# Attention of a three-stage kernel: a turn's first scores in two halves of the queries, and one turn with its products in another order

## The chip, the cores and the metric

The kernel runs on one core of a Trainium2 chip. The metric is the device time of one execution in microseconds (us); of several runs the median is given.

## The reference, cut to what matters

Three stages follow one another: an attention with fading scores and no softmax, and two feed-forward layers over its output.

```
scores = q @ k.T / sqrt(64)                      # 4 batches, 8 heads, 576 positions, 64 wide
ret    = scores * gamma_h ** (i - j) for i >= j  # else 0
x      = (ret @ v) as 2304 tokens x 512
x      = prelu(x @ w_in, alpha) @ w_out          # 512 -> 2048 -> 512
out    = silu1.702(x @ w2_in) @ w2_out           # h * sigmoid(1.702 h)
```

Inputs and outputs are float32. The change is in the attention alone.

## The kernel before, in words

**The attention's tiling.** The 32 pairs of batch and head are worked two heads at a time: 16 turns, one for each entry of `PAIRS`. A turn's two heads lie in the two halves of the 128 partitions (`halves`, 0 to 63 and 64 to 127). The 576 positions are cut into four chunks of 128 and a tail of 64. Within a chunk the scores are computed and multiplied by a table of fades; across chunks the sum of keys times values is carried as a state, as a linear attention does.

**A turn's products on TensorE**, all made by the helper `mm` (L353), in program order:

- `a_scores` writes the tiles `sc`, one for each head: for each of four chunks and each head one product, weights 64 rows x 128 columns (the keys), 128 queries streamed. The two heads use different row halves of the array.
- `a_outer` writes `st`: keys times values of each chunk, weights 128 x 64. The keys come from `kts`, which `a_keys` has scaled on ScalarE (two instructions, one for each head, L317) after its DMA.
- `a_within` writes `av` of the turn before: the faded scores `r` times the values, weights 128 x 64, 128 queries streamed.
- `a_tail` (tile `st`), then `a_across` (tile `av`), weights 64 x 64: the tail's state, and states times queries for the turn before.

The first turn (i = 0) and the second (i = 1) differ: turn i = 0 does its own `a_within`, and turn i = 1 does none. "The fourth turn" is i = 3.

**Beside them**: `a_evac` (VectorE, L385) multiplies `sc` by the table into `r`; `a_states` and `a_sums` (ScalarE, VectorE) turn `st` into the states that `a_across` of the next turn reads; `a_out` copies the result away; GpSimd scales the queries (`a_queries`). `sc` has three buffers, `av` two.

**What sets the order.** The order on each engine is that in which the program issues instructions (`manual_schedule`). Between the steps of a turn `run_to` issues what is due of a list of events: the loading and the splitting of the first layer's weights. After 16 turns and one more for the rest come the first layer (L514, L555) and the second (L696), whose products follow one another in fixed order.

An `mm` on float32 leaves two product records (MATMUL) and two weight-load records (LDWEIGHTS) in the trace, so the 8 products of a turn's scores are 16 records of each kind. The products of the two heads run side by side, so the 16 records come in 8 pairs.

Of the kernel before, what the change touches and what calls it, by code (L numbers as in the profile page):

```python
# [46 lines left out]
def kernel(  # L47
# [68 lines left out]
    def run_to(time):  # L116
        while events and events[0][0] <= time:
            _, _, fn, args = events.pop(0)
            fn(*args)
# [180 lines left out]
    halves = (slice(0, 64), slice(64, 128))  # L300
# [32 lines left out]
    def a_tables(p):  # L333
        def table(o, c0, n, row, key):
            nc.vector.scalar_tensor_tensor(
                out=tab_sb[o, p, c0:c0 + n], in0=row, scalar=vtab_sb[o, p, key:key + 1],
                in1=mask_sb[o, o.start:o.start + n], op0=ALU.mult, op1=ALU.mult,
            )

        for e in range(2):  # L340
            table(slice(0, 128), e * 128, 128, query(p, e), e)
        for e, o in enumerate(halves):
            table(o, 256, 64, query(p, e, o, 64), 4)

    def a_otab(p):
        for e, o in enumerate(halves):
            copy(tab_sb[o, p, 320:448], query(p, e, o))
        o = tab_sb[:, p, 320:768]
        copy(o[:, 128:256], o[:, 0:128])
        copy(o[:, 256:448], o[:, 0:192])  # L350

    def mm(out, lhsT, rhs, start, stop):
        return nc.tensor.matmul(  # L353
            out=out, lhsT=lhsT, rhs=rhs, start=start, stop=stop, skip_group_check=True
        )

    def a_keys(i):
        n = kts(i).rearrange("p (j n) -> p j n", j=4)
        for e, o in enumerate(halves):
            scale(n[:, :, o], n[:, :, o], vtab_sb[:, PAIRS[i][1], e:e + 1])  # L360
        k_t[i] = n

    def a_scores(i, chunks=range(4)):
        q, k = ld[i][0:2]
        if i not in sc_t:
            sc_t[i] = [aps.tile([128, 512], F32, tag="sc", name="sc", bufs=3) for _ in halves]
        t = sc_t[i]
        for j in chunks:
            for e, o in enumerate(halves):
                mm(t[e][:, j * 128:j * 128 + 128], k[j][o], q[j][o], j == 0, True)  # L370

    def a_tail(i):
        q, k = ld[i][0:2]
        for o in halves:
            mm(s_t[i][o, 0:64], k[4][o], q[4][o], i == 0, True)

    def a_outer(i):
        t, v, n = s_t[i], ld[i][2], k_t.pop(i)
        for j in range(4):
            for e, o in enumerate(halves):  # L380
                mm(t[o, j * 64 + 64:j * 64 + 128], n[:, j, o], v[:, 2 * j + e], i > 0 and j == 0, True)

    def a_evac(i):
        for e, t in enumerate(sc_t.pop(i)):
            nc.vector.tensor_tensor(  # L385
                out=r_t[i][0][:, e].rearrange("p (j n) -> p j n", j=4),
                in0=t.rearrange("p (j n) -> p j n", j=4),
                in1=tab_sb[:, PAIRS[i][1], e * 128:e * 128 + 128].rearrange(
                    "p (a n) -> p a n", a=1).to_broadcast([128, 4, 128]),
                op=ALU.mult,  # L390
            )

    def a_queries(i):
        behind = latest[0]
        r = tmp("r", i, [128, 2048])
        r_t[i] = (
            r[:, 0:1024].rearrange("p (e n) -> p e n", e=2), r[:, 1024:1536],
            r[:, 1088:1600].rearrange("p (b n) -> p b n", b=2)[:, :, 0:64], r[:, 1600:2048],
        )
        ins = nc.gpsimd.tensor_tensor(  # L400
            out=r_t[i][3], in0=ld[i][3], in1=tab_sb[:, PAIRS[i][1], 320:768], op=ALU.mult
        )
        if behind:
            tc.add_manual_dep(ins.ins, behind.ins.name, SYNC, reason="beside the products of the scores")

    def a_states(i):
        p = PAIRS[i][1]
        s = r_t[i][1]
        scale(s[:, 0:320], s_t.pop(i)[:, 0:320], vtab_sb[:, p, 2:3])

    def a_sums(i):
        p = PAIRS[i][1]
        s = r_t[i][1]
        nc.vector.scalar_tensor_tensor(
            out=s[:, 320:512], in0=s[:, 64:256], scalar=vtab_sb[:, p, 2:3], in1=s[:, 128:320],
            op0=ALU.mult, op1=ALU.add,
        )
        half = r_t[i][2]
        nc.vector.scalar_tensor_tensor(
            out=s[:, 384:512].rearrange("p (b n) -> p b n", b=2), in0=half,  # L420
            scalar=vtab_sb[:, p, 3:4], in1=s[:, 384:512].rearrange("p (b n) -> p b n", b=2),
            op0=ALU.mult, op1=ALU.add,
        )
        latest[0] = nc.vector.tensor_tensor(
            out=s[:, 0:64], in0=s[:, 0:64], in1=tab_sb[:, p, 256:320], op=ALU.mult
        )

    def a_within(i):
        v, r = ld[i][2], r_t[i][0]
        t = aps.tile([128, 1024], F32, tag="av", name="av", bufs=2)  # L430
        av_t[i] = t, [t[:, A0 + j * 128:A0 + j * 128 + 128] for j in range(4)] + [t[:, A0 + 512:A0 + S]]
        for j in range(4):
            for e, o in enumerate(halves):
                mm(av_t[i][1][j][o], v[:, 2 * j + e], r[:, e, j * 128:j * 128 + 128], j % 2 == 0, True)

    def a_across(i):
        out, v = av_t[i][1], ld[i][2]
        _, s, _, q = r_t.pop(i)
        for c in range(1, 5):
            s0 = 64 if c == 1 else 192 + c * 64  # L440
            for o in halves:
                mm(out[c][o], s[o, s0:s0 + 64], q[o, c * 128 - 128:min(c * 128, 448)], False, True)
        for o in halves:
            mm(out[4][o], v[o, 8], s[o, 0:64], False, True)

    def a_out(i):
        b, p = PAIRS[i]
        t = av_t.pop(i)[0][:, A0:A0 + S]
        ld.pop(i)
        s0 = 0  # L450
        for c in range(2):
            n0, n1 = max(CH[c][0] - b * S, 0), min(CH[c][1] - b * S, S)
            if n0 >= n1:
                continue
            if (c, p) not in x_t:
                x_home(c, p, xp[c])
            o = b * S - CH[c][0]
            x = x_t[c, p][:, :, n0 + o:n1 + o]
            copy(x[:, 0], t[:, n0:n1])
            rests.append((x, t[:, n0:n1]))  # L460
            s0 = n1
        if s0 < S:
            n = i - NP
            if n // 3 not in xs_t:
                xs_t[n // 3] = tmp("xs", n // 3, [128, 3, S])
            copy(xs_t[n // 3][:, n % 3, s0:S], t[:, s0:S])
# [3 lines left out]
    def a_rests():  # L470
        while rests:
            x, t = rests.pop(0)
            sub(nc.vector, x[:, 1], t, x[:, 0])
# [452 lines left out]
    with tc.manual_schedule():  # L926
# [24 lines left out]
        for i in range(n_a + 1):  # L951
            j = i - 1
            if i < n_a:
                a_scores(i)
                a_queries(i)
                a_evac(i)
            if i in (1, 2):
                a_tables(i + 1)
            a_rests()
            run_to(i)  # L960
            if i < n_a:
                s_t[i] = aps.tile([128, 512], F32, tag="st", name="st")
                if i == 0:
                    a_tail(i)
                a_outer(i)
                if i == 0:
                    a_states(i)
                    a_tables(1)
            if i != 1:
                a_within(max(j, 0))  # L970
            if 0 < i < n_a:
                a_tail(i)
                a_states(i)
            if i < n_a:
                a_sums(i)
            if i + 1 < n_a:
                a_keys(i + 1)
            if i == 0:
                a_otab(1)
            run_to(i + 0.25)  # L980
            if i:
                a_across(j)
                a_out(j)
            if i in (1, 2):
                a_otab(i + 1)
            for n in (3, 4) if i == 0 else (i + 4,):
                if n < n_a:
                    a_load(n)
            if i == 0:
                nc.sync.dma_start(out=alpha_sb, in_=alpha)  # L990
            run_to(i + 0.75)
# [49 lines left out]
        for r in range(R):  # L1041
            z = r * 2 * NU
            for j in range(NJ):
                u = z + 7 * j
                for t, what in (
# [3 lines left out]
                    if r == 0 and j in (5, 6) and what in ("g22", "g12"):  # L1049
                        t = 8.01  # L1050
# [114 lines left out]
```

## Time and profile before

| what | value |
|---|---|
| median of 3 runs | 800.93 us (800.91 to 801.43) |
| the profiled execution | 800.28 us, of which its span 798.6 us |
| TensorE busy, products | 793.6 us, 99% of the span |
| TensorE busy, weight loads | 740.2 us, 93% |
| VectorE, ScalarE, GpSimd busy | 80%, 66%, 10% |
| turns 2 to 16 of the attention | from 9.12 us to 63.59 us |

The span runs from the first instruction of the profile to the last one; the execution is 1.7 us longer than it. Product records of TensorE are pipelined and their ends are modelled, so a record's start says more than its length. "Chain" is the work that ended last, followed back from the last instruction. In the chain a piece of an engine is listed from the end of the piece before it.

### The profile page before, as it was taken

The page shows a single profiled execution, that of the slowest core. Times are in us where ns is not written, and L with a number is a line of the kernel's source. Part 1 is how long each engine was busy: PE and PEld are TensorE (multiplying, and loading weights), DVE is VectorE, ACT ScalarE, POOL GpSimd, SP SyncE. Part 2 cuts the span into 40 slices and gives each one's busy share as a digit, 9 for nine tenths or more (in the row PEclk, how much of TensorE's full clock was granted, in tenths as well). Part 3 has the DMA queues.
Part 4 walks back from the last instruction along what each step waited for, and adds up shares of the span by engine and source line. Part 5 has one row for each costly group of instructions (what it writes and reads, how often), then busy time and mean ns, then how long its engine had stood idle before and what let it go on. Part 6 is the DMA issues. An engine that isn't in the chain of part 4 may idle for free.

```text
span 798.6 us, 14132 instructions
## 1 busy us (share of the span) xinstructions
PE 793.6 (99%) x5004; PEld 740.2 (93%) x5004; DVE 642.1 (80%) x1195; ACT 527.9 (66%) x959; POOL 83.5 (10%) x104
## 2 busy tenths in 40 slices
PE   9999999999999999999999999999999999999998
PEld 8998888888888888999999999999999999999997
DVE  7888987888467576879999899799677898787775
ACT  7689869885536856556678666676566675666552
POOL 2230112100022003626100000000000000000000
PEclk9999999999999999999999999999999999999999
DMA  9998999755889966797989556986435985536771
GB/s 351 417 386 333 327 352 342 286 217 209 294 278 401 360 224 227 253 337 254 337 323 355 177 174 233 343 295 235 147 125 193 323 312 187 159 120 232 267 278 60
DMA packets 87789, 214.08 MB, mean 268 GB/s; under 512 B 7971, under 2 KB 43811, under 8 KB 79014
## 3 DMA queue, kind: packets, MB, share of 16 engines
q1 hardware_dynamic: 80784, 187.99, 65.6%
q0 software_dynamic: 6784, 25.17, 9.0%
q8 instruction: 39, 0.64, 0.3%
q14 instruction: 32, 0.26, 0.1%
q10 hardware_dynamic: 150, 0.02, 0.0%
HBM read 152.59 MB, written 60.56 MB: 267 GB/s over the span
## 4 chain that ended last, share of the span: by engine, by line
PE 98%; DMA 1%; DVE 0%; issue 0%
PE acc L696 33%; PE h L696 25%; PE acc L555 16%; PE h L514 16%; PE av L353 4%; PE sc L353 2%; PE st L353 2%; DMA ws<-sm 1%; PE wps L942 0%; PE dq L326 0%; DVE c L178 0%; DVE wz L930 0%
## 5 line engine op out<-in xcount | busy, mean ns | idle before, releaser
L108 DVE TENSOR_TENSOR gsf<-g,gsf 128x384 fp32r<-128x384 f32 (+1 forms) x272 | 156.4, 586 | 54.5 <-ACT gsf L103 53.1
L103 ACT ACTIVATE gsf<-g 128x384 fp32r<-128x384 f32 (+1 forms) x272 | 145.8, 542 | 75.6 <-PE acc L696 32.8
L555 PE MATMUL acc<-gsf,wo 128*128 128x512 f32 x576 | 138.2, 389 | 0.0
L514 PE MATMUL h<-x,wi 128*128 128x512 f32 x576 | 138.2, 389 | 0.0
L696 PE MATMUL acc<-gsf,ws 128*128 128x384 f32 x768 | 135.1, 334 | 0.2 <-DMA ws<-sm 0.2
L696 PEld LDWEIGHTS acc<-gsf,ws 128*128 128x128 f32 x768 | 133.2, 188 | 0.5 <-ACT x L103 0.5
L555 PEld LDWEIGHTS acc<-gsf,wo 128*128 128x128 f32 x576 | 108.1, 188 | 22.8 <-ACT raw L103 0.3
L514 PEld LDWEIGHTS h<-x,wi 128*128 128x128 f32 x576 | 108.1, 188 | 22.5
L696 PE MATMUL acc<-x,ws 128*128 128x384 f32 x660 | 128.3, 334 | 0.0
L696 PEld LDWEIGHTS acc<-x,ws 128*128 128x128 f32 x660 | 115.5, 188 | 0.2 <-ACT tm L103 0.2
L696 PE MATMUL h<-x,ws 128*128 128x384 f32 x540 | 107.7, 334 | 0.0
L696 PE MATMUL h<-gsf,ws 128*128 128x384 f32 x576 | 101.9, 334 | 0.0
L696 PEld LDWEIGHTS h<-gsf,ws 128*128 128x128 f32 x576 | 100.0, 188 | 0.2 <-issue 0.2
L696 PEld LDWEIGHTS h<-x,ws 128*128 128x128 f32 x540 | 94.8, 188 | 0.0
L178 DVE TENSOR_TENSOR tm<-h,tm 128x384 f32<-128x384 f32 x97 | 53.6, 553 | 26.9 <-PE h L696 21.5
L178 DVE TENSOR_TENSOR g<-g 128x384 f32<-128x384 f32 x114 | 63.0, 553 | 0.7
L103 ACT ACTIVATE tm<-acc 128x384 f32<-128x384 f32 x62 | 30.4, 491 | 48.0 <-PE acc L696 46.4
L522 DVE SCALAR_TENSOR_TENSOR g<-g,rise_sb,h 128x512 f32<-128x512 f32 (+1 forms) x49 | 36.4, 742 | 29.7 <-ACT g L527 29.5
L527 ACT ACTIVATE g<-h 128x512 f32<-128x512 f32 (+1 forms) x49 | 29.1, 593 | 40.5 <-PE h L514 39.9
L178 DVE TENSOR_TENSOR raw<-raw 128x256 f32<-128x256 f32 x116 | 45.6, 433 | 1.0
L148 DVE SCALAR_TENSOR_TENSOR raw<-raw 128x1024 int32<-128x1024 int32 x32 | 39.3, 1229 | 2.6 <-ACT raw L141 2.6
L129 POOL DMA_DIRECT2D raw<-in_w_dram x44 | 23.2, 534 | 173.2 <-DVE raw L178 52.9
(104 smaller groups left out, 922.9 us busy)
## 6 DMA issues: line engine op xcount, KB each, us to landing
ws<-sm SPq DMA_DIRECT2D x32, 1024.0 KB, 7.0
ws<-sp SPq DMA_DIRECT2D x24, 1024.0 KB, 5.5
raw<-in_w_dram POOLq DMA_DIRECT2D x44, 512.0 KB, 7.5
sm<-raw SPq DMA_DIRECT2D x32, 512.0 KB, 4.3
pad<-rg SPq DMA_DIRECT2D x48, 256.0 KB, 2.7
ld<-in_qkv_dram SPq DMA_DIRECT2D x13, 864.0 KB, 7.9
raw<-in_w_dram SPq DMA_DIRECT2D x20, 512.0 KB, 8.9
r<-raw SPq DMA_DIRECT2D x16, 512.0 KB, 2.9
```

Of the source, the lines that this page charges most:

```text
L103: return nc.scalar.activation(out=out, in_=in_, func=ACTF.Copy)
L108: latest[0] = eng.tensor_tensor(out=out, in0=a, in1=b.bitcast(F32), op=ALU.subtract)
L129: eng.dma_start(out=raws[key][:, c * DM:c * DM + DM], in_=f[:, c * DM:c * DM + DM])
L148: latest[0] = nc.vector.scalar_tensor_tensor(out=g[:, 0:2 * DM], in0=t[:, :, 1], scalar=3, in1=t[:, :, 0], op0=ALU.logical_shift_left, op1 ...
L178: latest[0] = (eng or nc.vector).tensor_tensor(out=out, in0=x, in1=y, op=op)
L353: return nc.tensor.matmul(out=out, lhsT=lhsT, rhs=rhs, start=start, stop=stop, skip_group_check=True)
L514: nc.tensor.matmul(out=t, lhsT=w[:, cw, k * 128:k * 128 + 128], rhs=x[:, cx], start=(i == 0), stop=(i == 3 * NK - 1),)
L522: nc.vector.scalar_tensor_tensor(out=g[0], in0=g[1], scalar=rise_sb[:, m:m + 1], in1=h, op0=ALU.mult, op1=ALU.add)
L527: nc.scalar.activation(out=out, in_=in_, func=ACTF.Relu, scale=-1.0)
L555: nc.tensor.matmul(out=acc[0][d], lhsT=w[:, d // 2, cw, d % 2 * 128:d % 2 * 128 + 128], rhs=g[:, cx], start=(m == m0 and i == 0), stop=(m ...
L696: nc.tensor.matmul(out=out, lhsT=w(cw), rhs=x(cx), start=(start and n == 0), stop=True, skip_group_check=True,)
```

## The change

Two edits. In `a_scores`, for the first chunk of every turn but the first, each head's product of 128 queries is issued as two products of 64: first both heads on queries 0 to 63, then both heads on queries 64 to 127, with the same keys as weights. The flag that starts a new sum in the PSUM bank stays on the first half alone. In turn i = 3 `a_within` is issued in front of `a_outer` and not behind it.

```
         for j in chunks:
-            for e, o in enumerate(halves):
-                mm(t[e][:, j * 128:j * 128 + 128], k[j][o], q[j][o], j == 0, True)
+            for cols in halves if j == 0 and i else (slice(0, 128),):
+                for e, o in enumerate(halves):
+                    n = slice(j * 128 + cols.start, j * 128 + cols.stop)
+                    mm(t[e][:, n], k[j][o], q[j][o, cols], j + cols.start == 0, True)
...
                 if i == 0:
                     a_tail(i)
+                if i == 3:
+                    a_within(j)
                 a_outer(i)
...
-            if i != 1:
+            if i not in (1, 3):
                 a_within(max(j, 0))
```

TensorE at the head of turn i = 4, which stands for the turns i = 1 to 15, before (a shape is that of the output: partitions x columns):

```order
L353 MATMUL av<-r,ld 64x64 x2
L353 MATMUL sc<-ld 128x128 x8
L353 MATMUL st<-ld,kts 64x64 x8
L353 MATMUL av<-r,ld 64x128 x8
L353 MATMUL st<-ld 64x64 x2
```

The same place with the change:

```order
L353 MATMUL av<-r,ld 64x64 x2
L353 MATMUL sc<-ld 128x64 x4
L353 MATMUL sc<-ld 128x128 x6
L353 MATMUL st<-ld,kts 64x64 x8
L353 MATMUL av<-r,ld 64x128 x8
```

Two products of 128 queries have become four of 64; the six of the other chunks stand as before.

TensorE in turn i = 3, before (in brackets the engine or the DMA queue whose semaphore an instruction waits for):

```order
L353 MATMUL sc<-ld 128x128 [waits DMAHW4_49]
L353 MATMUL sc<-ld 128x128 [waits DVE_49]
L353 MATMUL sc<-ld 128x128 x6
L353 MATMUL st<-ld,kts 64x64 [waits DMAHW5_49,PE_49,Activation_49]
L353 MATMUL st<-ld,kts 64x64 [waits Activation_49]
L353 MATMUL st<-ld,kts 64x64 x6
L353 MATMUL av<-r,ld 64x128 [waits DVE_49]
L353 MATMUL av<-r,ld 64x128 x7
L353 MATMUL st<-ld 64x64 x2
```

The same turn with the change:

```order
L353 MATMUL sc<-ld 128x64 [waits DMAHW4_49]
L353 MATMUL sc<-ld 128x64 [waits DVE_49]
L353 MATMUL sc<-ld 128x64 x2
L353 MATMUL sc<-ld 128x128 x6
L353 MATMUL av<-r,ld 64x128 [waits DVE_49]
L353 MATMUL av<-r,ld 64x128 x7
L353 MATMUL st<-ld,kts 64x64 [waits DMAHW5_49,PE_49,Activation_49]
L353 MATMUL st<-ld,kts 64x64 [waits Activation_49]
L353 MATMUL st<-ld,kts 64x64 x6
L353 MATMUL st<-ld 64x64 x2
```

The eight products of `a_within` stand ahead of the two waits for ScalarE's scaled keys; the tail's two products stay behind both groups.

## Rows read from the trace of the kernel before

**Rows 1.** The page: busy shares (busy us, share, instructions), and the chain's shares.

```profile
PE 793.6 (99%) x5004; PEld 740.2 (93%) x5004; DVE 642.1 (80%) x1195; ACT 527.9 (66%) x959; POOL 83.5 (10%) x104
...
PE 98%; DMA 1%; DVE 0%; issue 0%
```

**Rows 2.** The chain in order of time, turns 4 and 5: start us, us, what.

```profile
15.71 1.09 PE sc L353 x16
16.80 0.80 PE st L353 x15
17.60 0.93 PE av L353 x16
18.53 0.26 PE st L353 x4
18.80 0.89 PE av L353 x20
19.68 1.09 PE sc L353 x16
20.78 0.61 PE st L353 x16
21.39 0.88 PE av L353 x16
22.27 0.26 PE st L353 x4
22.53 0.89 PE av L353 x20
23.42 1.09 PE sc L353 x16
```

**Rows 3.** Stretches: turn 1, turns 2 to 16, the rest.

```profile
core 0: us, PE busy (x) PEld busy (x) DVE busy (x) ACT busy (x) POOL busy (x), PEclk, DMA share, GB/s
...
9.12:63.59 54.47, 54.47 (x1049) 49.19 (x1050) 46.47 (x109) 42.14 (x91) 17.50 (x16) 1.00 1.02 404
```

**Rows 4.** Loads at the head of turn 6, three short windows: start us, us, what.

```profile
23.34 0.30 PEld L353 LDWEIGHTS sc<-ld 64*128 64x128 f32 x4
...
23.45 0.19 PEld L353 LDWEIGHTS sc<-ld 64*128 64x128 f32 x2
...
23.56 0.20 PEld L353 LDWEIGHTS sc<-ld 64*128 64x128 f32 x2
```

**Rows 5.** Products in turn 6, short windows, each from one pair's start on.

```profile
23.35 0.38 PE L353 MATMUL sc<-ld 64*128 64x128 f32 x2
...
23.56 0.39 PE L353 MATMUL sc<-ld 64*128 64x128 f32 x4
...
23.67 0.39 PE L353 MATMUL sc<-ld 64*128 64x128 f32 x4
...
24.44 0.28 PE L353 MATMUL st<-ld,kts 128*64 128x64 f32 x2
...
24.54 0.40 PE L353 MATMUL st<-ld,kts 128*64 128x64 f32 x8
...
24.60 0.40 PE L353 MATMUL st<-ld,kts 128*64 128x64 f32 x7
```

**Rows 6.** The tile `sc` in turns 2 to 16: duration ns min/median/max, first and last start.

```profile
L353 PEld LDWEIGHTS sc<-ld x240: 182/188/188, 9.1 to 61.5; 64*128 64x128 f32 x120
L353 PE MATMUL sc<-ld x240: 272/272/373, 9.1 to 61.6; 64*128 64x128 f32 x120
```

**Rows 7.** ScalarE around the outer products of turn 4, timeline.

```profile
16.02 0.91 ACT L317 ACTIVATE kts<-kts,vtab_sb 128x256 f32<-128x256 f32 x2 [0.57 <-DMA kts<-in_kn_dram]
16.83 0.69 ACT L103 ACTIVATE x<-av 128x512 fp32r<-128x512 f32 x2
```

**Rows 8.** TensorE's loads in turn 4, two windows of the timeline.

```profile
16.73 0.50 PEld L353 LDWEIGHTS st<-ld,kts 128*64 128x64 f32 x8
...
16.98 0.48 PEld L353 LDWEIGHTS st<-ld,kts 128*64 128x64 f32 x13
```

**Rows 9.** VectorE's evacuation of turn 3's scores, timeline.

```profile
13.88 1.28 DVE L385 TENSOR_TENSOR r<-sc,tab_sb 128x512 f32<-128x512 f32 x2
```

**Rows 10.** Waits of TensorE's loads, and of its products, whole span: us, times, longest.

```profile
PEld acc L696 <- ACT x L103: 0.5, 1, 0.5
PEld acc L555 <- ACT raw L103: 0.3, 1, 0.3
...
PE acc L696 <- DMA ws<-sm: 0.2, 1, 0.2
```

## The prediction

> **What bounds the kernel now.** I read the page's busy shares and chain first. TensorE is busy for 99% of the span and makes up 98% of the chain of work that ended last [rows 1]; the other engines hold nothing that counts. So a change on TensorE's own instruction stream is worth what it adds to or takes from that stream, at once and in full, unless a later wait gives some of it back. Next I read the stretch in which the change lies: from 9.12 to 63.59 us TensorE is busy all the time, at a granted clock of 1.00, which is the 2.4 GHz level [rows 3]. The DMA engines are also full there (share 1.02, 404 GB/s), yet TensorE does not wait for them. The chain by turns then shows a fixed beat: scores 1.09 us, outer products 0.61, `a_within` 0.88, tail 0.26, `a_across` 0.89 [rows 2]. Turn 5 goes from 19.68 to 23.42, 3.74 us. Turn 4 goes from 15.71 to 19.68, 3.97 us, so 0.23 us more, and the surplus stands in the outer products (0.80 for 0.61) and in `a_within` right after them.
>
> **How one pair of products runs.** Everything hangs on whether a product of 64 queries can go by faster than the load of its 128-column weights. The single starts at the head of turn 6 show it. Pairs of loads start at 23.34, 23.45 and 23.56 [rows 4]: 0.11 us for each. The first pair of products is issued at 23.35 but the second starts at 23.56, 0.21 later, while the third comes 0.11 behind that [rows 5]. So the first pair waits some 0.10 us for its weights, and only this once; later loads lie beside the products of the pair before. The records agree: the longest `sc` product has 373 ns against a median of 272, 101 more [rows 6]. The outer products, whose weights have 64 columns, show the same at half the size: the first pair starts at 24.44, the second at 24.54, the third at 24.60 [rows 5], so a beat of 0.06 and a first wait of about 0.05. A weight load for 128 columns thus takes 0.10 to 0.11 us, for 64 columns about 0.05. In a pair of 128 columns by 128 queries, load and product take nearly the same, and the beat (0.11) doesn't tell which of the two sets it. In the split pair they part: a product of 64 queries streams for about 0.05 us (the beat of `st`, which also streams 64 columns, is 0.06), but its load still has 128 columns.
>
> **Edit 1, the split, 15 turns.** It removes two products of 128 queries and adds four of 64: in pairs, two become four, because each half needs both records of its float32 product, and each record has a load of its own. (TensorE has as many load records as product records, 5004 each [rows 1], so a load is not left out when weights come again.) The weights alternate between the two records of a product, so the second half could not keep what is loaded in any case.
>
> - Upper end, if the load sets the beat: four loads of 0.11 where two were. By the starts 23.34 and 23.56, two loads are 0.22 us, so +0.22 a turn; 15 x 0.22 = 3.3 us. With the steady beat of turn 6 for each added pair (1.09 for eight pairs less 0.20 for the head leaves about 0.111), it is 15 x 2 x 0.111 = 3.3 us again.
> - Lower end, if loads could be hidden under something else: four pairs at the 0.06 of `st`, against two at 0.11, +0.02 a turn; 15 x 0.02 = 0.3 us.
>
> I take the upper end. The nearest rows are those of `sc` itself: its second load starts when the first has ended (23.34, 23.45), and its third when the second has (23.56), so a load isn't started two ahead, and nothing else is there to hide it under. VectorE evacuates `sc` later by the same 0.22, but TensorE needs the result only in the next turn: in turn 3 the evacuation ended at 15.16 (13.88 + 1.28) [rows 9], and its reader, `a_within`, starts at 17.60 in turn 4 [rows 2]. No DMA is moved by this edit. The waits at a turn's head (the loaded `ld`, a free buffer of `sc`) move with the first product and cost nothing today.
>
> By the Trainium skill ("TensorE: Matmul & The Clock Gate", section "LDWEIGHTS (loading the stationary operand)") a load takes its columns divided by 1.2 GHz, whatever its rows, so about 107 ns for 128 columns; as an estimate by that page, 15 x 2 x 0.107 = 3.2 us. The trace agrees (0.11 from start to start) [rows 4]. By the same page's section "Back-to-back issue gap", taken for a lone product, the columns streamed alone set the beat, which would speak for the lower end; no row here has short products on long loads.
>
> **Edit 2, turn 4.** The outer products need keys that ScalarE scales in two instructions, 16.02 to 16.93, after waiting 0.57 us for their DMA [rows 7]. TensorE's loads for them start at 16.73, and the pairs run only from 16.98 on [rows 8]: the second head's keys came 0.25 us late, which is the surplus of turn 4 (0.23). With the change `a_within` comes first: 0.88 us of products whose input was ready at 15.16 [rows 9]. The outer products then start at about 17.6 plus 0.66 for the splits of turns 2 to 4, over 1 us behind the keys. The stall goes: -0.23 us. The splits alone would nearly have done this: three of them shift the outer products by 0.66 us, and the keys come by DMA; so edit 2 is worth nothing on top of edit 1, and I count the stall once. What is behind the moved products: the tail's products come last before and after, so ScalarE's reading of `st` starts no later within the turn; both groups have weights of 128 x 64, so the shapes on TensorE change as often as before. The phase between the two heads, which the late keys broke, stays whole, with no price seen (0.93 against 0.88, inside the 0.23).
>
> **What comes after.** All of the first and second layer moves back by the sum. TensorE waits there three times for other engines or transfers, 0.5, 0.3 and 0.2 us [rows 10]. Their inputs come over full DMA queues during the attention or out of long queues on ScalarE, so 3 us more head start may shorten them; or they move along. Bounds -1.0 and 0; I take 0, since two of the three are deep in the second layer, where buffers come free by TensorE's own progress.
>
> **Sum.** The profiled execution has 800.28 us (its span 798.6 and 1.7 around it); +3.3 - 0.23 = 803.35. It lies 0.65 below the median of the runs, so the forecast is 800.93 + 3.07 = 804.0 us, 0.38% slower. Its own range is 803.0 (all later waits gone) to 804.6 (the keys' wait stays, and 0.02 us more per turn).
>
> **Rivals.**
>
> - *Streaming sets the beat.* The load of 128 columns is hidden better than the rows let me see, and the four short pairs take 0.06 each: +0.3 - 0.23, so 801.0 us, no change. For it: in steady pairs load and product tie, so no row shows a load as the sole bound. Against it: the first pair's wait of 0.10.
> - *The head of a turn gets shorter.* The one exposed load in a turn (0.10 us, 23.35 to 23.56 less a beat) would shrink if the first short product made room earlier for what follows: at the most 15 x 0.10 = 1.5, and the stall of 0.23, so 800.93 - 1.7 = 799.2 us, faster. It decides from the point where a turn's second score pair starts less than 0.16 us behind the first and the added pairs still cost nothing. Against it: the first load's length doesn't depend on the queries, and the second is there already when the first ends.
> - *Load and product in the same rows don't overlap when the product is short.* Then each of four pairs costs 0.11 + 0.05, against two of 0.11 now: +0.42 a turn, 15 x 0.42 = 6.3, less 0.23: 807.0 us. Against it: the loads that start at 23.45 lie beside the products that run until 23.56 [rows 4, 5]. The Trainium skill ("TensorE: Matmul & The Clock Gate", section "The mechanism") has loads overlap products in flight only where the row group differs; here the load for the same half of the rows does overlap, so the trace does not bear that rule out.
>
> **How the numbers follow.** Forecast 0.77, streaming 0.12, shorter head 0.06, no overlap 0.05. A measurement of this kernel can tell about 0.2%, 1.6 us, from no change (799.3 to 802.5). The forecast and the last rival are slower, 0.80 with a little lost to partly hidden loads; streaming and those partial cases are the same, 0.14; the shorter head is faster, 0.06. The forecast's own range alone leaves out about a quarter, so the range reaches down to the streaming case: 800.8 to 804.6 us.
>
> **What would show it.** In the profile after: `sc` pieces of the chain of 1.31 us instead of 1.09 in turns 2 to 16; at a turn's head five pairs of loads in a row 0.11 apart, with products of 64 queries at the same distance; 60 records more of each kind (15 turns, two more products, two records each); turn 4 as long as turn 5, with no wait for ScalarE. The streaming case would show the short pairs 0.06 apart; the shorter head a smaller first gap. I am wrong if `sc` still takes about 1.1 us, or if a wait between turns takes the added time back.

## The result, and the profile after

| | before | changed | difference |
|---|---|---|---|
| first comparison, median of 8 and 8 runs | 801.43 us (800.13 to 803.47) | 805.54 us (803.85 to 808.73) | +4.1 us, ratio 1.0055 [1.0036, 1.0075] |
| second, 15 and 5 runs | 801.38 us | 804.82 us (804.54 to 805.11) | +3.4 us, ratio 1.0042 [1.0029, 1.0054] |
| third, 24 and 6 runs | 801.86 us | 804.32 us (803.71 to 805.20) | +2.5 us, ratio 1.0028 [1.0016, 1.0040] |
| forecast | 800.93 us (3 runs) | 804.0 us (800.8 to 804.6) | +3.07 us |

A ratio stands with its 95% interval and is not the quotient of the two medians. The change is slower, as forecast, but the time of the first comparison lies 0.9 us above the range. The three comparisons put the difference at 4.1, 3.4 and 2.5 us, on both sides of the forecast's 3.07, and their intervals overlap, so the first question is what scatters.

The profiled execution of the changed kernel, on its page, against [rows 1]:

```profile
PE 800.2 (99%) x5064; PEld 746.7 (93%) x5064; DVE 642.1 (80%) x1195; ACT 527.9 (65%) x959; POOL 83.3 (10%) x104
...
PE 98%; DMA 2%; SPq 0%; DVE 0%; issue 0%; ACT 0%
```

TensorE has 60 records more of each kind, as forecast; the other engines have the same work. The chain of the changed kernel in turns 4 and 5 (start us, us, what), the rows that answer to [rows 2]:

```profile
20.36 1.32 PE sc L353 x20
21.67 1.02 PE av L353 x16
22.70 0.72 PE st L353 x20
23.42 0.89 PE av L353 x20
24.31 1.31 PE sc L353 x20
25.62 0.61 PE st L353 x16
26.24 0.88 PE av L353 x16
27.11 0.26 PE st L353 x4
27.38 0.89 PE av L353 x20
28.26 1.32 PE sc L353 x20
```

The scores take 1.31 or 1.32 us where they took 1.09, and everything else in turn 5 is what it was. Turn 5 goes from 24.31 to 28.26, 3.95 us for 3.74; the mean over turns 5 to 14 is 3.956 for 3.733, so 0.223 more. At the head of turn 6 the loads stand as they stood in [rows 4], only that the products beside them are short (three short windows of the timeline):

```profile
28.19 0.30 PEld L353 LDWEIGHTS sc<-ld 64*128 64x128 f32 x4
...
28.30 0.19 PEld L353 LDWEIGHTS sc<-ld 64*128 64x128 f32 x2
...
28.41 0.31 PEld L353 LDWEIGHTS sc<-ld 64*128 64x128 f32 x4
```

Each pair of loads comes 0.11 us after the one before: the load sets the beat.

But this execution's span is 7.9 us longer (806.5 for 798.6), not 3. Its chain in the first three turns:

```profile
2.18 5.29 DMA ld<-in_qkv_dram
...
7.61 1.22 PE st L353 x15
8.82 1.81 PE av L353 x16
10.63 2.44 PE sc L353 x20
13.07 1.46 PE st L353 x20
14.53 1.71 PE av L353 x20
16.24 1.48 PE sc L353 x20
```

and that of the kernel before:

```profile
8.06 1.06 PE av L353 x16
9.12 1.09 PE sc L353 x16
10.21 0.88 PE st L353 x20
11.09 0.89 PE av L353 x20
11.98 1.09 PE sc L353 x16
```

The first turn, which the change doesn't touch, waited here for a load that landed at 7.47 us. Then the products of turn 2 ran at little more than half pace: 1.46 for 0.88 us (`st`), 1.71 for 0.89 (`av`). The granted clock, by its record in the trace, reached 2.4 GHz at 16.5 us, where it was there at 8.1 us in the profile before. (The record begins with this rise, and the view of the stretches prints 1.00 ahead of it too; that the clock was at its lower level until then, 1.2 GHz, is read from the pace of the products.) Summed by turns from the two chains: the start and the clock cost 4.2 us (1.5 until turn 2, 2.5 in turn 2, 0.2 in turn 3, each without its split), the split 3.35 (15 times 0.223), the fourth turn gave back 0.25, turn 15 was 0.08 longer than its neighbours, and the layers after the attention took 0.5 more. That is the 7.9.

### The profile page after: what moved, and what is told of

Its sections match the earlier page's. It is cut to its first block, busy times and chain, and to the rows that moved or that the text cites. A ratio compares the mean times of both kernels' runs of the same rounds, so it can differ in the third digit from the quotient of the medians.

```text
span 806.5 us, 14252 instructions
## 1 busy us (share of the span) xinstructions
PE 800.2 (99%) x5064; PEld 746.7 (93%) x5064; DVE 642.1 (80%) x1195; ACT 527.9 (65%) x959; POOL 83.3 (10%) x104
## 4 chain that ended last, share of the span: by engine, by line
PE 98%; DMA 2%; SPq 0%; DVE 0%; issue 0%; ACT 0%
PE acc L698 32%; PE h L698 25%; PE acc L557 16%; PE h L516 16%; PE av L353 4%; PE sc L353 3%; PE st L353 2%; DMA pad<-rg 1%; DMA ld<-in_qkv_dram 1%; SPq L309 0%; DVE c L178 0%; SPq L311 0%; ACT gsf L103 0%; SPq L687 0%
```

## The experiments

In the diffs, turns are counted from i = 0 as in the code.

**1. The changed kernel twice more.** No edit.

> The changed kernel once more, beside the kernel before on the same chip. Theory S (start): the part of the loss beyond 3.1 us came from the start of single executions (in the profile after, the first turn's values landed late and the granted clock stayed at 1.2 GHz until 16.5 us, 8.1 us in the one before), which hits either kernel by chance: the difference of the medians over more runs comes to 3.1 to 3.7 us, and a profile whose second turn starts near 9.1 us has turns of 3.95 us and a span of about 802. Theory W (a later wait): the shift of 3.1 us opens a wait in the second layer (1.2 us for ScalarE's gsf near 448 us in the profile after) in every execution: the difference stays at 4.0 us or more and the wait is in this profile too.

> The changed kernel a third time. By the terms measured so far (15 turns x 0.226, the fourth turn's stall of 0.24 gone or replaced by one of up to 0.17) the difference is 3.1 to 3.3 us; with the start's chance 3.0 to 3.8. Rival: 4.0 or more again, as in the first comparison; then something in the change lengthens the start.

Measured: +3.4 and +2.5 us (table above). The two profiles have turns of 3.95 to 3.96 us, a second turn that starts (first load of `sc`) at 9.98 and 9.74 us, and a clock that is up at 10.1 and 9.5 us. So +4.1 was not the change's own size: that single executions differ in their start, as theory S has it, is borne out by these profiles. But the loads, which theory S names with the clock, are not needed for it. In the second of the two profiles TensorE waits for no load in the first turn, and its products there start when those of the kernel before do; only the last group takes 1.76 us for 1.06, most of it at the lower clock:

```profile
6.59 1.46 PE st L353 x20
8.05 1.76 PE av L353 x16
9.81 1.32 PE sc L353 x20
```

The second run of experiment 5, without a split, shows the same (1.89 us, the clock up at 10.2). So the clock rises later in some executions with no pause of TensorE ahead of it; why is open. The wait in the second layer (theory W) was there in all three, with 1.2, 0.6 and 1.3 us at TensorE's loads (for `gsf`, `x` and `gsf` of ScalarE); experiment 2 shows that the kernel before has it too.

These profiles also show what I had not counted on, a wait in the fourth turn. TensorE's loads in the first of the two runs (who waited for whom, us, times, longest):

```profile
PEld av L353 <- DVE x L108: 0.3, 1, 0.3
```

The turn took 4.13 us, not 3.95, in both runs.

**2. The kernel before as a control.** No edit, but a profile of its own.

> The kernel before, unchanged, as a control with a profile of its own. Theory S: its executions differ among themselves by when the first turn's values and keys land; a second profile has the second turn's start somewhere between 9.0 and 10.6 us and the clock's rise between 8 and 16 us, and a fourth turn near 3.97 us; ratio 1.000. Rival: it starts at 9.1 us with the clock up at 8.1 us as in the first profile, so late starts belong to the changed kernels.

Measured: ratio 0.9996 [0.9986, 1.0006]. The start was early (second turn at 9.16 us, clock up at 8.4 us), so this run alone does not show late starts without the change. Waits of TensorE's loads and products in it:

```profile
PEld acc L696 <- ACT gsf L103: 0.9, 1, 0.9
...
PE acc L696 <- DMA ws<-sm: 0.7, 1, 0.7
```

In [rows 10] these were 0.5 and 0.2 us. The second layer's wait therefore comes without the change too, and differs from one execution to the next.

**3. The split alone.**

```
-                if i == 3:
-                    a_within(j)
                 a_outer(i)
...
-            if i not in (1, 3):
+            if i != 1:
```

> The split alone, the order of the fourth turn as before. By the prediction the split adds 0.22 us to each of 15 turns, and the added time covers the late keys of the fourth turn, so the move of a_within is worth nothing on top: the fourth turn takes 3.95 us like the others, no wait for ScalarE's keys stands in it, and the time is that of the whole change within 0.3 us. Rival: the keys come later too (ScalarE waits for TensorE's scores ahead of them), the stall of 0.23 us stays, and the fourth turn takes 4.2 us.

Measured: 804.82 us against 801.38, ratio 1.0050 [1.0036, 1.0063], the same median as both edits together. The chain in its fourth turn:

```profile
16.09 1.32 PE sc L353 x20
17.41 0.61 PE st L353 x16
18.02 0.88 PE av L353 x16
18.90 0.26 PE st L353 x4
19.16 0.89 PE av L353 x20
20.05 1.32 PE sc L353 x20
```

3.96 us, with no wait left in it: three splits have covered the late keys, as the prediction said. It is even shorter than with the move (4.13). The times can't show that 0.17 us: the five runs lie between 804.4 and 806.7 us.

**4. The move alone.** The kernel before with `a_within(j)` in front of `a_outer(i)` for i = 3, and no split.

> The move of a_within in the fourth turn alone, no split. By the prediction it covers the late keys with 0.88 us of products: the fourth turn takes 3.74 us instead of 3.97, the outer products run without a wait, and the kernel is 0.2 us faster, which is near what a measurement can tell (0.03%). Rival: the moved products wait themselves, or the next turn's states come later, and turn 4 or 5 takes 0.2 us more or longer: no gain or a loss.

Measured: 801.87 us, ratio 1.0006 [0.9997, 1.0015], no gain. The fourth turn took 4.36 us, the rival's number. Its chain:

```profile
16.90 0.83 DVE x L108 x2
...
17.78 1.09 PE av L353 x16
18.87 0.72 PE st L353 x20
```

and the waits of TensorE's loads there:

```profile
PEld av L353 <- DVE x L108: 0.8, 1, 0.8
```

The moved products do not wait for the faded scores. They wait for VectorE's subtractions that read an older `av` tile: `av` has two buffers, and `a_within` of turn 3 writes the one that turn 1's result still occupies. In the kernel before these stand on VectorE behind four table instructions:

```profile
15.08 1.40 DVE L335 SCALAR_TENSOR_TENSOR tab_sb<-fade_sb,vtab_sb,mask_sb 128x128 f32<-128x128 f32 x4
16.49 0.82 DVE L108 TENSOR_TENSOR x<-av,x 128x512 fp32r<-128x512 f32 x2
```

They end at 17.31, just ahead of the products that need the buffer.

**5. The move, with the subtractions ahead of the tables.**

```
+            if i == 2:
+                a_rests()
             if i in (1, 2):
                 a_tables(i + 1)
             a_rests()
...
+                if i == 3:
+                    a_within(j)
                 a_outer(i)
```

> The kernel before with a_within moved in the fourth turn, and with the two subtractions of a_rests issued ahead of the four tables on VectorE in turn i = 2 (not behind them). Theory R (after the move alone took 4.36 us for its fourth turn): the moved products wait for VectorE's subtractions of turn 1's output, which still read the av buffer that they write; the subtractions now end 1.4 us earlier (the four table instructions), so the wait goes, the late keys are covered too, and the fourth turn takes 3.74 us; 0.24 us less than before, within what a measurement can tell. Rival: they wait for the evacuation of scores (L385), which this edit doesn't touch: the fourth turn stays at 4.2 to 4.4 us.

> The move together with the earlier subtractions once more: by its fourth turn alone (3.73 for 3.97 us) 0.24 us faster. It was 0.95 us faster in its first comparison; if that was more than chance in the start, the ratio comes to 0.9985 to 0.9990 again; by the fourth turn alone it is 0.9997.

VectorE and TensorE in the first of the two, timeline:

```profile
15.52 0.81 DVE L108 TENSOR_TENSOR x<-av,x 128x512 fp32r<-128x512 f32 x2
16.25 1.09 DVE L335 SCALAR_TENSOR_TENSOR tab_sb<-fade_sb,vtab_sb,mask_sb 128x128 f32<-128x128 f32 x4
```

```profile
15.62 1.16 PE L353 MATMUL sc<-ld 64*128 64x128 f32 x16
16.72 1.09 PE L353 MATMUL av<-r,ld 128*64 128x128 f32 x16
17.64 0.64 PE L353 MATMUL st<-ld,kts 128*64 128x64 f32 x16
```

The fourth turn took 3.73 us in both runs: the wait for the buffer and the wait for the keys are gone. Theory R holds. The times were 800.80 against 801.75 (ratio 0.9986 [0.9977, 0.9995]) and 801.74 against 801.86 (0.9996 [0.9986, 1.0006]). The second agrees with 0.24 us by the fourth turn alone; that the fourth turn gets shorter is seen in both traces, that the kernel beats the one before in one of two comparisons of the times. The 0.95 us of that one is four times what the fourth turn gives; the rest is not explained by the edit.

**6. Quarters in place of halves.**

```
-            for cols in halves if j == 0 and i else (slice(0, 128),):
+            for cols in [slice(c, c + 32) for c in range(0, 128, 32)] if j == 0 and i else (slice(0, 128),):
```

> The first chunk as four products of 32 queries for each head instead of two of 64 (turns 2 to 16), the fourth turn as in the change. Theory L (the load of 128 key columns sets the beat, whatever is streamed): six pairs are added to a turn at 0.11 us each, 0.66 us a turn, so the scores take 1.75 us in the chain and the kernel is 15 x 0.66 - 0.23 = 9.7 us slower than before. Rival (streamed columns with a fixed price for each pair, here 0.11 by chance at 64): pairs of 32 queries go by faster, at 0.08 us or less, and the loss is 15 x (8 x 0.08 - 0.22) - 0.23 = 6 us or less.

Measured: 811.57 us against 801.38, +10.2 us, ratio 1.0126 [1.0112, 1.0140]. A turn's scores in the chain:

```profile
22.12 1.76 PE sc L353 x28
```

0.67 us more than before for six added pairs, 0.11 each, though a product now streams 32 queries and not 64. The number of loads sets the time and the number of queries does not: the load sets the beat. Nor is 0.11 a price of any pair, whatever is loaded: the pairs of `st`, with 64 columns loaded and 64 streamed, go by at 0.06 [rows 5]. Three turns of this profile were longer than the rest (4.50, 4.69 and 4.96 for 4.40 us), some 0.95 us in all, of which the chain lists 0.34 under "issue"; with it the sum of 9.7 comes to 10.6, and 10.2 was measured.

**7. A later start.** The kernel before, with two small transfers ahead of all loads.

```
+        for _ in range(2):
+            nc.sync.dma_start(out=rise_sb, in_=alpha)
         for i in range(3):
             a_load(i)
```

> The kernel before with two small transfers (8 KB each) issued ahead of all loads on the sync engine's queue, so that every load of the first turn starts about 0.9 us later. Theory S (the spread comes from the start): TensorE pauses in the first turn for its values and keys, as in the profile of the changed kernel; the second turn starts at 10 us or later, and the granted clock rises later than the 8.1 us of the profile before, up to 16.5; the time grows by 1 to 4 us although no later instruction changed. Rival: only the 0.9 us itself is lost, the clock rises at 8 to 9 us as before, and the time grows by less than 1 us.

Measured: 804.05 us against 801.75, +2.3 us, ratio 1.0025 [1.0015, 1.0035]. Its chain:

```profile
0.81 1.74 DMA rise_sb<-in_alpha_dram
...
2.95 0.43 SPq L309
...
4.36 4.55 DMA ld<-in_qkv_dram
...
11.97 1.71 PE sc L353 x16
```

The edit did more than it was meant to: the two small transfers write the same tile, the second waited 1.74 us for the first, and the first load was issued at 2.95 us where it had been at 0.81, 2.1 us later and not 0.9. The second turn's scores then come 2.85 us later (11.97 for 9.12) and take 1.71 us for 1.09, since the clock was up at 13.2 us only; the first layer's products begin 3.4 us later. So late loads in the first turn cost more than their own delay in this execution, in the way of theory S, but by how much a delay of 0.9 us would have cost this run doesn't tell, and the rival as it was put isn't decided.

**8. An earlier load for the first turn.** Experiment 5 with the first turn's values issued from ScalarE's queue.

```
+            q = nc.scalar if (i, n) == (0, 2) else nc.sync
+            q.dma_start(out=t[:, c0:c1], in_=qkv[b, p, :, c0:c1])
```

> As the run with the move and the earlier subtractions, and with the first turn's values loaded from ScalarE's queue instead of the sync engine's, behind its two small loads. Theory S: the values land earlier, later loads are issued 0.43 us earlier each, the pause in the first turn goes, the second turn starts at 9.1 us in every execution, and the median falls by 0.5 to 1 us against the kernel before, with a smaller spread. Rival: ScalarE issues the load later than the sync engine would, or the transfer takes a share of the queues from the first turn's keys: the same pause stands at the keys and nothing is gained.

Measured: 803.52 us against 801.75, ratio 1.0018 [1.0009, 1.0027]: slower. The load was issued earlier and landed later, after 6.92 us:

```profile
1.84 6.92 DMA ld<-in_qkv_dram
8.77 0.09 issue
```

My expectation fell. The first turn's keys came late too, as the rival has it: ScalarE began to scale them at 8.05 us, after a wait of 2.34, and at 5.98 in the profile before. Why the load takes longer from that queue was not settled; the run shows that late loads in the first turn can move the total by 2 us.

## Why the prediction was right, and where it failed

- **What bounds the kernel: right.** All added TensorE time appeared in the total. In the split alone the first layer began 3.0 us later: the 3.35 of the split, less the keys' 0.24 and a second turn that started 0.07 earlier.
- **Edit 1, the split: right in mechanism and in size.** "I take the upper end", 0.22 a turn and 3.3 us in all; the turns give 0.223 and 3.35. Quarters confirm that the beat is the load's. The streaming rival falls (the scores rose by 0.22), and so does the rival without overlap: a load that could not lie beside its product would have made it +0.42 a turn. The sign named for the shorter head did come: at the head of turn 6 the second pair of products starts 0.16 us behind the first where it was 0.21 [rows 5] (the changed kernel, two short windows).

```profile
28.20 0.33 PE L353 MATMUL sc<-ld 64*128 64x64 f32 x2
...
28.36 0.39 PE L353 MATMUL sc<-ld 64*128 64x64 f32 x4
```

But the loads kept their 0.11, so the smaller gap saved nothing. One reading in the prediction doesn't hold: "its second load starts when the first has ended (23.34, 23.45)". The load records are 182 to 188 ns long [rows 6] and start 0.11 us apart, so by the records two pairs of loads lie side by side. The rows show the beat of the loads, not where one ends.
- **Edit 2, the fourth turn: wrong in its step.** The prediction put it so: "With the change `a_within` comes first: 0.88 us of products whose input was ready at 15.16". Their input was ready, but the place for their output was not. The wait that the order prints on that product names VectorE, and I took it for the evacuation of the scores [rows 9]; it was for the subtractions that free the `av` buffer, at 17.31 in that trace. Alone, the move makes the fourth turn 0.39 us longer (4.36 for 3.97). Behind the splits TensorE comes later, and the wait is 0.17 us (4.13 for 3.96) or none (3.95 in the profile after). That edit 2 is worth nothing on top of edit 1 came out nearly right, since the splits alone do cover the keys; but the move is not free, it costs 0 to 0.17 us.
- **What comes after: 0 is not contradicted, the bounds were wrong.** The layers behind the attention took 732.1 us in the profile before and 732.3 in the control, 732.6, 732.1 and 732.8 in three of the changed kernel and 733.2 in the split alone. Over all twelve profiles they lie between 731.5 and 733.2, and I had allowed for nothing above 0.
- **The sum and its range: the step that put the time outside.** "It lies 0.65 below the median of the runs, so the forecast is 800.93 + 3.07 = 804.0 us", with an own range to 804.6 "(the keys' wait stays, and 0.02 us more per turn)". That upper end is made of terms of the two edits alone; what differs from one execution to the next was put at nothing, in the base, in the first turn and in the layers after. The base was the median of three runs; over the 47 runs of the three comparisons it is 801.49 us, 0.56 higher, and single executions of the kernel before, in all comparisons, lie between 800.1 and 804.1. With 3.35 for the split, -0.24 to -0.07 for the fourth turn and that base the sum is 804.6 to 804.8; the median over 19 runs of the changed kernel is 804.95. The first comparison's 805.54 lies 0.8 us above even that sum. Its one profile lost 4.2 us at the start, but the other seven executions have none, so whether the start is what lifted their median stays open.

**Left open:** whether the changed kernel starts late more often. No instruction ahead of the second turn was changed, and kernels without the split started late too (second turn at 9.87 us in the second run of experiment 5, 9.46 in experiment 4). But the profiles with a split have it at 10.56, 9.98, 9.74, 9.72 and 8.98 us, those without at 9.05, 9.16, 9.46, 8.99 and 9.87 (experiments 7 and 8 left out); five of each don't tell. The later comparisons ran on three chips, each beside the kernel before; which chip the first ran on is not on record.

## What to carry to other kernels

Cutting a product along its streamed side saves nothing where its weights take as long to load as the streaming does, as here (0.11 us for either): every piece pays the whole load again, so count loads, not columns. Before a product is moved ahead, look up what its output buffer waits for as well as its inputs, and read which instruction of the named engine it is. And give a range room for the scatter of single executions, above all at the start, which here hung on the first transfers and on when the clock rose.

## What the runs showed of the hardware that I had not expected

- A second turn that began 1.5 us later went with 4.2 us lost by the fourth: TensorE, which had paused for its loads in the first turn, was granted the lower clock (1.2 GHz) until 16.5 us and not until 8.1: `st` took 1.46 us for 0.88, `av` 1.71 for 0.89. In two other executions the clock rose at 9.5 and 10.2 us with no pause for a load before it.
- A load issued from ScalarE's queue, a little earlier than from the sync engine's (1.84 for 2.19 us), landed late (8.77 us), with 6.92 us from issue to landing; from the sync engine's queue it took 4.55 to 5.29 us in three profiles.
- In the one profile of the quarters three turns were 0.10, 0.29 and 0.56 us longer than the others, with nothing that the profile shows to wait for. Whether the short products brought it, one trace does not tell.
